# Five token blocks instead of six in a fused window-attention and two-FFN kernel, with the attention placed at quarters of a unit

## The chip, the cores and the metric

One core of a Trainium2 chip runs the whole program in one launch. The metric is the device time of that launch in microseconds (us); a time is the median of several runs. Engines are named as the profile names them: PE multiplies matrices (PEld loads its weights), DVE is the vector engine, ACT the scalar engine, POOL the third elementwise engine, SP issues most of the DMAs.

## The reference

4 sequences of 576 tokens, 8 heads of 64; a causal window of 64 keys; then two feed-forward nets over the 2304 tokens.

```python
scores = (q @ k.T) / sqrt(64)                  # per batch and head
scores = where(0 <= row - col < 64, scores, -1e9)
attn = softmax(scores)                         # max subtracted first
x = (attn @ v), heads side by side             # 2304 x 512
x = ((x @ w1) * (x @ w2) @ w3) @ w_out         # 512 -> 1024 -> 1024 -> 512
h = x @ w_in                                   # 512 -> 2048
out = (h * sigmoid(h)) @ w_out2                # 2304 x 512
```

## The kernel before

**Precision.** Most products are taken in three passes (`PASSES`): each operand is held as a high part and a low part, and PE adds high x high, high x low and low x high. So everything that feeds PE is copied (high part, on ACT) and subtracted (low part, on POOL or DVE). The weights come as float64 words and are turned into such pairs on the chip ("chunks", `steps_to`).

**Stages.** `phase_w` multiplies w3 and w_out into one 1024 x 512 matrix `wp`, so the first net is (a * b) @ wp. `phase_a(blk, hooks)` runs the first net for one block of tokens, `NB = 384` at a time, six blocks. It has 24 units of 12 matmuls. Units 0 to 15 make a = x@w1 and b = x@w2 in turn (line 520, tile `ab`): after an even unit ACT copies the accumulator into `a` (L526), after an odd one DVE multiplies (L528), ACT casts the product to its high part and POOL takes the low part (L79, L82, tiles `p` and `q`). Units 16 to 23 multiply by `wp` (line 540, tile `x`); ACT copies the result out and issues its DMA to the buffer `x2d`. The last block carries the conversion of the second net's weights. After it the second net runs over blocks of 512 tokens (L640, L659).

**Attention.** It is cut into 72 groups g, each 128 queries of two heads (18 token tiles of 128, 4 head pairs). A group is spread over six "halves" (`half(h)`); half 2g is its even one, 2g+1 its odd one. Even half 2g: PE takes the scores of g (L268 or L272, L276, tile `s`), multiplies the probabilities of group g-2 with the values (L349, L350, tile `o`) and transposes those of g-1 (L315, tile `t`). DVE adds the mask and takes the row minimum (L282, `sm`, `nm`), ACT copies the transposed probabilities of g-1 (L325, L327, `pt`), DVE takes their low parts (L328, L330), and ACT takes the exponentials of g (L293). Odd half 2g+1: DVE normalises g (L301, L303, L305), ACT and DVE add up group g-2's output (L357 to L360, `ot`) and POOL stores it (L361, `xr`), then q, k and v of later groups are split (L247, L251, L254, `qkhi`, `klo`, `vhl`). The first 17 groups (`plain`) take the scores in plain float32 with fewer of these steps.

**Order.** Nothing is scheduled automatically: each engine runs its instructions in the order in which the program emits them, and waits only for what an instruction needs. In `phase_w` 28 halves are emitted. In blocks 0 to 4 each of the 24 units emits one half ahead of its 12 matmuls (`halves_to(W_HALVES + 24 * blk + n + 1)`); in block 5 nothing is left. The tile `t` has one buffer, `sm` and `pt` have two. The next block's input is split out of `xr` during units 17 to 22 (`split_x`).

## Time and profile before

| | before |
|---|---|
| median of 3 runs | 861.66 us (861.57 to 862.0) |
| the profiled execution's own time | 861.8 us |
| its span in the trace | 860.0 us |
| PE busy | 842.0 us, 98% of the span |
| ACT, DVE, POOL busy | 497.7, 435.8, 445.0 us |
| `phase_w` (0 to 95.9 us) | PE busy 82.27 us of 96 |
| blocks 0 to 4 with attention (95.9 to 412.2) | a group every 5.25 us |
| block 5 (412.2 to 464.9), weights converted beside it | PE busy all of it |
| second net (464.9 to 860) | PE busy 391 us of 395 |

A row of the timeline gives start and length in us, engine, line, operation, what is written and read, and in brackets the idle time ahead of it with what ended it. The chain of waits is followed back from the last instruction: each piece is what the end of the program waited for at that time.

### The profile page before, as it was taken

What the parts mean: (1) busy time and instruction counts of PE and PEld (TensorE: products, weight loads), DVE (VectorE), ACT (ScalarE), POOL (GpSimd) and SP (SyncE); (2) the same over time, 40 slices, a digit from 0 to 9 for tenths busy, and PEclk for the clock granted to TensorE, in tenths of its full rate; (3) what the DMA queues carried; (4) which work ended last, traced back from release to release, by engine and by line L of the source; (5) the groups of instructions that cost most, each with busy time, mean ns of one, the idle gap of its engine ahead of it and who ended that gap; (6) DMA issues with size and microseconds to landing.
All of it is one profiled execution on the core that took longest, in us unless ns stands there. A gap on an engine that the chain in (4) does not pass through costs nothing.

```text
span 860.0 us, 13396 instructions
## 1 busy us (share of the span) xinstructions
PE 842.0 (98%) x4362; PEld 736.7 (86%) x4362; DVE 435.8 (51%) x1160; ACT 497.7 (58%) x1243; POOL 445.0 (52%) x494
## 2 busy tenths in 40 slices
PE   5899999999999999999999999999999999999998
PEld 2455799999999999999999888888888888888896
DVE  5979877677777777676465985111111111111111
ACT  5889778788788788787666874222222222222222
POOL 4668666566666666665595886223322232223222
PEclk9999999999999999999999999999999999999999
DMA  8988333333333334330687200200020002000100
GB/s 289 349 272 276 104 105 102 121 93 108 114 93 111 111 94 125 111 94 30 233 326 263 116 1 0 98 1 1 0 98 1 1 0 74 1 1 0 50 1 26
DMA packets 43205, 85.84 MB, mean 100 GB/s; under 512 B 4864, under 2 KB 22528, under 8 KB 43136
## 3 DMA queue, kind: packets, MB, share of 16 engines
q1 hardware_dynamic: 37088, 75.55, 26.7%
q10 hardware_dynamic: 6048, 9.44, 3.0%
q8 instruction: 35, 0.57, 0.3%
q14 instruction: 34, 0.28, 0.1%
HBM read 75.53 MB, written 9.44 MB: 99 GB/s over the span
## 4 chain that ended last, share of the span: by engine, by line
PE 86%; DVE 1%; ACT 1%; issue 1%; POOLq 0%; POOL 0%; ACTq 0%; DVEq 0%
PE h L640 23%; PE o L659 23%; PE ab L520 22%; PE x L540 12%; PE t L315 2%; PE o L349 1%; PE s L272 1%; PE s L276 1%; PE o L350 1%; ACT sm L293 0%; DVE a L528 0%; DVE sm L305 0%; DVE cv_b L128 0%; POOLq L765 0%; DVE hl L144 0%
## 5 line engine op out<-in xcount | busy, mean ns | idle before, releaser
L82 POOL TENSOR_TENSOR g<-sg,g 128x512 fp32r<-128x512 f32 (+1 forms) x80 | 94.7, 1184 | 244.8 <-ACT g L79 217.7
L640 PE MATMUL h<-x2t,hl 128*128 128x512 f32 (+1 forms) x960 | 210.1, 368 | 0.0
L659 PE MATMUL o<-hl,g 128*128 128x512 f32 x864 | 209.7, 390 | 0.1
L640 PEld LDWEIGHTS h<-x2t,hl 128*128 128x128 f32 x960 | 169.3, 188 | 31.2
L646 DVE TENSOR_TENSOR sg<-h,sg 128x512 f32<-128x512 f32 (+1 forms) x80 | 51.1, 638 | 283.7 <-ACT sg L645 283.6
L659 PEld LDWEIGHTS o<-hl,g 128*128 128x128 f32 x864 | 161.1, 188 | 33.5 <-POOL g L82 0.5
L645 ACT ACTIVATE sg<-h 128x512 f32<-128x512 f32 (+1 forms) x80 | 44.4, 555 | 190.0 <-PE h L640 189.7
L520 PE MATMUL ab<-xa,hl 128*128 128x384 f32 x576 | 119.0, 341 | 0.0
L520 PE MATMUL ab<-xb,hl 128*128 128x384 f32 x576 | 115.3, 334 | 0.0
L520 PEld LDWEIGHTS ab<-xb,hl 128*128 128x128 f32 x576 | 101.2, 188 | 0.0
L520 PEld LDWEIGHTS ab<-xa,hl 128*128 128x128 f32 x576 | 99.2, 188 | 0.0
L132 POOL TENSOR_TENSOR cv_b<-cv_b,cv_r 128x512 int32<-128x512 int32 x48 | 73.5, 1531 | 19.1 <-DVE cv_b L128 8.1
L79 ACT CAST g<-sg 128x512 fp32r<-128x512 f32 (+1 forms) x80 | 46.3, 579 | 63.5 <-DVE sg L646 63.5
L361 POOL TENSOR_TENSOR xr<-ot 128x128 f32<-128x128 f32 x55 | 31.6, 575 | 98.3 <-DVE ot L360 67.2
L251 POOL TENSOR_TENSOR klo<-qk,qkhi 64x192 fp32r<-64x192 f32 x110 | 67.4, 613 | 7.6 <-ACT qkhi L247 2.7
L540 PE MATMUL x<-p,wp 128*128 128x384 f32 x360 | 68.0, 339 | 0.0
L293 ACT ACTIVATE sm<-sm,nm 128x192 f32<-128x192 f32 x144 | 64.5, 450 | 3.9 <-DVE nm L282 2.5
L540 PEld LDWEIGHTS x<-p,wp 128*128 128x128 f32 x360 | 61.7, 188 | 0.1
L125 DVE TENSOR_SCALAR cv_z<-cv_b 128x512 int32<-128x512 int32 x72 | 49.4, 686 | 15.7 <-ACT cv_b L114 14.7
L114 ACT ACTIVATE cv_b<-words 128x512 f32<-128x512 f32 x72 | 48.3, 671 | 12.2 <-DMA words<-in_w_out 4.6
L128 DVE SCALAR_TENSOR_TENSOR cv_b<-words,cv_z 128x512 int32<-128x512 int32 x72 | 49.5, 687 | 3.3
L115 ACT ACTIVATE cv_r<-words 128x512 int32<-128x512 uint32 x72 | 47.8, 664 | 0.0
(81 smaller groups left out, 1236.5 us busy)
## 6 DMA issues: line engine op xcount, KB each, us to landing
qk<-in_qkv SPq DMA_DIRECT2D x55, 384.0 KB, 3.1
words<-in_w_out SPq DMA_DIRECT2D x24, 512.0 KB, 8.0
words<-in_w3t SPq DMA_DIRECT2D x16, 512.0 KB, 6.4
words<-in_w SPq DMA_DIRECT2D x16, 512.0 KB, 6.4
words<-in_w_in SPq DMA_DIRECT2D x16, 512.0 KB, 6.7
v<-in_qkv SPq DMA_DIRECT2D x55, 96.0 KB, 2.7
x2d<-x2s ACTq DMA_DIRECT2D x24, 192.0 KB, 1.9
out_x<-osb ACTq DMA_DIRECT2D x18, 256.0 KB, 2.1
```

Source lines behind the costliest of these rows:

```text
L82: (nc.vector if eng_lo == "dve" else nc.gpsimd).tensor_tensor(out=lo, in0=src, in1=f32(hi), op=ALU.subtract)
L114: nc.scalar.activation(out=f32(self.b), in_=f32(self.high), func=AF.Copy, scale=2.0**-112)
L125: nc.vector.tensor_scalar(out=self.z, in0=b, scalar1=3, scalar2=None, op0=ALU.logical_shift_left)
L128: nc.vector.scalar_tensor_tensor(out=b, in0=self.high, scalar=-0x80000000, in1=self.z, op0=ALU.bitwise_and, op1=ALU.bitwise_or)
L132: nc.gpsimd.tensor_tensor(out=x, in0=b, in1=self.r, op=ALU.add)
L251: nc.gpsimd.tensor_tensor(out=k_lo[g % 2][hs, h * 192 : h * 192 + 192], in0=t[hs, n], in1=f32(hi[hs, n]), op=ALU.subtract)
L293: nc.scalar.activation(out=x, in_=x, func=AF.Exp, scale=-1.0, bias=nm[:, h : h + 1], accum_out=sums_of[g % 2][:, h, 0:1])
L520: nc.tensor.matmul(acc, lhsT=w[:, l, fs], rhs=x[k // 2][:, k % 2, r, :], start=(k == 0 and n == 0), stop=(k == 3 and n == 2),)
L540: nc.tensor.matmul(acc, lhsT=wp[f][:, l, o * 128 : (o + 1) * 128], rhs=p[f][:, r, :], start=(f == 0 and n == 0), stop=(f == 7 and n == 2),)
L640: nc.tensor.matmul(acc, lhsT=weights["in", f // 4, k][:, l, fs], rhs=x[:, k, r, :], start=(k == 0 and i == 0), stop=(k == 3 and i == 2),)
L646: nc.vector.tensor_tensor(out=sg, in0=acc, in1=sg, op=ALU.mult)
L659: nc.tensor.matmul(oacc[t], lhsT=g[:, l, t * 128 : (t + 1) * 128], rhs=weights["out", f][:, r, :], start=(f == 0 and i == 0), stop=(f == 1 ...
```

## The change

**Blocks.** `UNITS = (3, 3, 4, 4, 4)` gives five blocks of 384, 384, 512, 512 and 512 tokens instead of six of 384. Every matmul of `phase_a` in the last three is 512 columns wide, and the slots `p`, `q`, `xa`, `xb` and `xr` grow to 512 columns. To make room, `klo` and `kp` share one slot each (`klo` is allocated and zeroed on POOL when the first split group needs it, in block 0), and plain and split values share one.

**Halves.** The 120 halves that were 24 in each of five blocks are now 28, 28, 32 and 32 in four (`HALVES_AT`), and none in the last. They are placed at quarters of a unit, that is ahead of every 3 matmuls, by `attend(n, k)`.

**Order inside the halves.** In the even half the exponentials of g are emitted ahead of the copies of g-1's probabilities. The low parts of g-1 move to the odd half, behind the normalising of g.

```diff
-        def unit(n):
-            halves_to(W_HALVES + 24 * blk + n + 1)
+        def attend(n, k):
+            halves_to(begun + min(ahead, -(-ahead * (4 * n + k + 1) // (96 if blk == 0 else 92))))
+
+        def unit(n):
+            attend(n, 0)
             hooks(n)
...
             for k in range(4):
                 w = weights["12", (2 * m + f // 4) * 4 + k]
+                if k:
+                    attend(s, k)
...
-            if 1 <= g <= NG:
-                split_t(g - 1, transposes(g - 1))
+            t_ps = transposes(g - 1) if 1 <= g <= NG else None
             if g < NG:
                 exps(g)
+            if t_ps is not None:
+                lows.append(split_t(g - 1, t_ps))
...
             if g < NG:
                 normalise(g)
+            if lows:
+                lows.pop()()
             if sums:
                 sums.pop()()
```

The blocks are counted from 0. PE in block 1, units 2 and 3, before. The names: `s`, `o` and `t` are scores, values and transposes, `ab` the products with w1 or w2.

```order
L315 MATMUL t_1972<-id_sb,sm_72 128x128 x3
L520 MATMUL ab_2_1984<-xa_1638,hl 128x384 x6
L520 MATMUL ab_2_1984<-xb_1639,hl 128x384 x6
L520 MATMUL ab_3_2020<-xa_1638,hl 128x384 x6
L520 MATMUL ab_3_2020<-xb_1639,hl 128x384 x6
L272 MATMUL s_2036<-qkhi_1932 128x192 x2
L276 MATMUL s_2036<-klo_74,qkhi_1932 128x384
L349 MATMUL o_2044<-pt_975,vhl_1937 128x256 x2
L350 MATMUL o_2044<-pt_973,vhl_1937 128x4x64
L315 MATMUL t_2048<-id_sb,sm_73 128x128 x3
L520 MATMUL ab_4_2060<-xa_1638,hl 128x384 x6
```

The rows of one group stand behind unit 3 there. PE in block 1 after, units 3 and 4:

```order
L329 MATMUL t_2140<-id_sb,sm_73 128x128 x3
L548 MATMUL ab_3_2124<-xa_1718,hl 128x384 x3
L548 MATMUL ab_3_2124<-xb_1719,hl 128x384 x6
L548 MATMUL ab_4_2185<-xa_1718,hl 128x384 x6
L548 MATMUL ab_4_2185<-xb_1719,hl 128x384 x3
L286 MATMUL s_2195<-qkhi_2101 128x192 x2
L290 MATMUL s_2195<-klo_1111,qkhi_2101 128x384
L367 MATMUL o_2203<-pt_982,vhl_2106 128x256 x2
L368 MATMUL o_2203<-pt_980,vhl_2106 128x4x64
L329 MATMUL t_2207<-id_sb,sm_72 128x128 x3
L548 MATMUL ab_4_2185<-xb_1719,hl 128x384 x3
```

The attention's five rows stood between whole units, 24 matmuls from one group to the next; now they stand inside unit 4, 18 matmuls after the last ones.

DVE in block 1 before, from the second row minimum of a group (`nm`) to the multiply of unit 7 (`a_3`); `rs` and `sm` are the normalising, `pt` the low parts, `ot` the output sums.

```order
L282 ISA sm_73,nm_2116<-s_2112,mask_sb 128x192
L282 ISA nm_2116 128x1
L328 TENSOR_TENSOR pt_975<-t_2124,pt_975 128x2x128
L330 TENSOR_TENSOR pt_973<-t_2124,pt_973 64x64 x2
L301 TENSOR_REDUCE rs_2117<-es_82 128x2
L303 RECIPROCAL rs_2117<-rs_2117 128x2
L305 TENSOR_TENSOR sm_73<-sm_73,rs_2117 128x384
L359 TENSOR_TENSOR ot_2154<-o_2120,ot_2154 64x256
L360 TENSOR_TENSOR ot_2154<-o_2120,ot_2154 64x256
L254 TENSOR_TENSOR qkhi_2160<-qk_2016,qkhi_2160 64x256
L528 TENSOR_TENSOR a_3_2149<-ab_7_2172,a_3_2149 128x384
```

The low parts stand ahead of the normalising there. DVE in block 1 after, from the second row minimum to the multiply of unit 5 (`a_2`):

```order
L296 ISA sm_73,nm_2199<-s_2195,mask_sb 128x192
L296 ISA nm_2199 128x1
L315 TENSOR_REDUCE rs_2200<-es_77 128x2
L317 RECIPROCAL rs_2200<-rs_2200 128x2
L319 TENSOR_TENSOR sm_73<-sm_73,rs_2200 128x384
L344 TENSOR_TENSOR pt_981<-t_2207,pt_981 128x2x128
L346 TENSOR_TENSOR pt_979<-t_2207,pt_979 64x64 x2
L377 TENSOR_TENSOR ot_2237<-o_2203,ot_2237 64x256
L378 TENSOR_TENSOR ot_2237<-o_2203,ot_2237 64x256
L267 TENSOR_TENSOR qkhi_2243<-qk_2109,qkhi_2243 64x256
L556 TENSOR_TENSOR a_2_2219<-ab_5_2221,a_2_2219 128x384
```

The two rows of low parts have moved from ahead of the three of normalising to behind them; the multiply still stands at the end of this group's rows here.

ACT in block 1 before, from one cast of a product (`p`) to the next; `pt` are the copies, `sm` the exponentials.

```order
L79 CAST p_1882<-a_2_2073 128x384
L325 CAST pt_975<-t_2124 128x2x128
L327 CAST pt_973<-t_2124 64x64 x2
L293 ACTIVATE sm_73,es_82<-sm_73,nm_2116 128x192 x2
L526 COPY a_3_2149<-ab_6_2136 128x384
L357 COPY ot_2154<-o_2120 64x256
L358 COPY ot_2154<-o_2120 64x256
L247 CAST qkhi_2160<-qk_2016 128x768
L79 CAST vhl_2165<-v_1942 128x3x64
L79 CAST p_1882<-a_3_2149 128x384
```

The exponentials stand behind the copies there. ACT in block 1 after, from the exponentials of one group to those of the next:

```order
L307 ACTIVATE sm_73,es_77<-sm_73,nm_2199 128x192 x2
L339 CAST pt_981<-t_2207 128x2x128
L341 CAST pt_979<-t_2207 64x64 x2
L554 COPY a_2_2219<-ab_4_2185 128x384
L375 COPY ot_2237<-o_2203 64x256
L376 COPY ot_2237<-o_2203 64x256
L260 CAST qkhi_2243<-qk_2109 128x768
L90 CAST vhl_2248<-v_2041 128x3x64
L90 CAST p_1986<-a_2_2219 128x384
L307 ACTIVATE sm_72,es_76<-sm_72,nm_2272 128x192 x2
```

The exponentials stood behind the three copies into `pt`; now they stand ahead of them.

## Rows read from the trace of the kernel before

**Rows 1.** The page, parts 1 and 6: busy us; loads with KB and us to landing.

```profile
PE 842.0 (98%) x4362; PEld 736.7 (86%) x4362; DVE 435.8 (51%) x1160; ACT 497.7 (58%) x1243; POOL 445.0 (52%) x494
...
qk<-in_qkv SPq DMA_DIRECT2D x55, 384.0 KB, 3.1
```

**Rows 2.** The chain in order of time: start us, length us, what.

```profile
235.06 4.17 PE ab L520 x24
...
412.21 33.28 PE ab L520 x192
...
475.83 2.72 PE h L640 x12
...
814.67 1.43 PE h L640 x12
```

**Rows 3.** Line 82, who waited for it: us, times. (POOL's low parts.)

```profile
PEld x L540: 1.2, 4
```

**Rows 4.** Timeline of DVE, block 2: one round of a group.

```profile
235.15 0.56 DVE L528 TENSOR_TENSOR a<-ab,a 128x384 f32<-128x384 f32 x1
235.63 0.35 DVE L282 CUSTOM_DVE_ANT_0 sm<-s,mask_sb 128x192 f32<-128x192 f32 x1
...
236.90 0.42 DVE L328 TENSOR_TENSOR pt<-t,pt 128x256 fp32r<-128x256 f32 x1 [0.64 <-ACT pt L327]
237.24 0.45 DVE L330 TENSOR_TENSOR pt<-t,pt 64x64 fp32r<-64x64 f32 x2
237.91 0.16 DVE L301 TENSOR_REDUCE rs<-es 128x2 f32<-128x4 f32 x1 [0.22 <-ACT sm L293]
...
238.31 0.56 DVE L305 TENSOR_TENSOR sm<-sm,rs 128x384 f32<-128x384 f32 x1
239.24 0.42 DVE L359 TENSOR_TENSOR ot<-o,ot 64x256 f32<-64x256 f32 x1 [0.38 <-ACT ot L358]
...
240.03 0.42 DVE L254 TENSOR_TENSOR qkhi<-qk,qkhi 64x256 fp32r<-64x256 f32 x1
240.48 0.56 DVE L528 TENSOR_TENSOR a<-ab,a 128x384 f32<-128x384 f32 x1
```

**Rows 5.** The same stretch on ACT.

```profile
235.75 0.52 ACT L79 CAST p<-a 128x384 fp32r<-128x384 f32 x1 [0.83 <-DVE a L528]
236.17 0.36 ACT L325 CAST pt<-t 128x256 fp32r<-128x256 f32 x1
...
236.89 0.46 ACT L293 ACTIVATE sm<-sm,nm 128x192 f32<-128x192 f32 x1
...
237.90 0.48 ACT L526 COPY a<-ab 128x384 f32<-128x384 f32 x1
...
238.40 0.37 ACT L357 COPY ot<-o 64x256 f32<-64x256 f32 x1
...
239.16 0.83 ACT L247 CAST qkhi<-qk 128x768 fp32r<-128x768 f32 x1
```

**Rows 6.** The same stretch on PE: scores and values.

```profile
239.06 0.37 PE L272 MATMUL s<-qkhi 128*128 128x192 f32 x2
239.27 0.36 PE L276 MATMUL s<-klo,qkhi 128*128 128x384 f32 x1
239.46 0.39 PE L349 MATMUL o<-pt,vhl 128*128 128x256 f32 x2
```

**Rows 7.** Timeline of block 2, units 18 and 19: POOL and DVE at once.

```profile
274.28 1.02 POOL L82 TENSOR_TENSOR xa<-xr,xa 128x384 fp32r<-128x384 f32 x1
...
274.95 0.77 DVE L305 TENSOR_TENSOR sm<-sm,rs 128x384 f32<-128x384 f32 x1
```

**Rows 8.** Timeline of the start of block 0, conversions beside it: POOL, DVE, PE.

```profile
95.03 0.20 POOL L556 MEMSET pt<- 64x128 f32 x1
...
112.04 0.98 DVE L305 TENSOR_TENSOR sm<-sm,rs 128x384 f32<-128x384 f32 x1
...
113.17 0.52 PE L315 MATMUL t<-id_sb,sm 128*128 128x128 f32 x3 [0.30 <-DVE sm L305]
```

More of the change, by code (lines that the diff above doesn't have):

```diff
@@ L22 @@
 DM, FF, FF2 = 512, 1024, 2048
-NB = 384
-NBLK = T // NB
 NU = T // 128
+UNITS = (3, 3, 4, 4, 4)
+NBLK = len(UNITS)
+FIRST = [sum(UNITS[:b]) for b in range(NBLK + 1)]
+NBM = max(UNITS) * 128
 NPAIR = H // 2
@@ L32, with place @@
 W12_BY = [n * W12_A // 8 for n in range(8)] + [W12_A + n * (W12_B - W12_A) // 8 for n in range(8)]
+def place(g):
+    b = max(n for n in range(NBLK) if FIRST[n] * NPAIR <= g)
+    c, r = divmod(g - FIRST[b] * NPAIR, UNITS[b])
+    return b, FIRST[b] + r, c
 def mask_kind(u):
@@ L193, in tile_window_attention_ffn @@
     sm = [att.tile([128, 2, 192], F32, name=f"sm{i}", tag=f"sm{i}", bufs=1) for i in range(2)]
-    k_lo = [att.tile([128, 384], F32R, name=f"klo{i}", tag=f"klo{i}", bufs=1) for i in range(2)]
-    k_p = [att.tile([128, 384], F32, name=f"kp{i}", tag=f"kp{i}", bufs=1) for i in range(2)]
-    v_p = [att.tile([128, 320], F32, name=f"vp{i}", tag=f"vp{i}", bufs=1) for i in range(3)]
+    k_p = [att.tile([128, 384], F32, name=f"kp{i}", tag=f"k{i}", bufs=1) for i in range(2)]
+    k_lo = {}
     sums_of = [
@@ L219, in load_qk @@
             loaded.add(g)
-            u, c = place(g)
+            _, u, c = place(g)
             if not plain(g):
@@ L234, in load_v, with zero_beside @@
             loaded.add(("v", g))
+            v_raw[g] = att.tile([128, 320], F32, name=f"v{g}", tag="v", bufs=3)
             if plain(g):
-                nc.sync.dma_start(out=v_p[g % 3], in_=vp[g])
+                nc.sync.dma_start(out=v_raw[g], in_=vp[g])
                 return
-            v_raw[g] = att.tile([128, 3, 64], F32, name=f"v{g}", tag="v", bufs=3)
-            u, c = place(g)
-            nc.sync.dma_start(out=v_raw[g].rearrange("p t d -> p (t d)"), in_=qkv[u, c, :, 768:960])
+            _, u, c = place(g)
+            nc.sync.dma_start(out=v_raw[g][:, 0:192], in_=qkv[u, c, :, 768:960])
+    def zero_beside(t):
+        for h, hs in HEADS:
+            nc.gpsimd.memset(t[hs, 192 - h * 192 : 384 - h * 192], 0.0)
     def prep_qk(g):
@@ L245, in prep_qk @@
         t = qk_raw.pop(g)
+        if g % 2 not in k_lo:
+            k_lo[g % 2] = att.tile([128, 384], F32R, name=f"klo{g % 2}", tag=f"k{g % 2}", bufs=1)
+            zero_beside(f32(k_lo[g % 2]))
         hi = att.tile([128, 768], F32R, name=f"qkhi{g}", tag="qkhi", bufs=2)
@@ L327, in split_t, with low @@
             nc.scalar.copy(out=a[hs, h, 0], in_=before[hs])
-        nc.vector.tensor_tensor(out=b[:, :, 1, :], in0=own, in1=f32(b[:, :, 0, :]), op=ALU.subtract)
-        for h, hs in HEADS:
-            nc.vector.tensor_tensor(out=a[hs, h, 1], in0=before[hs], in1=f32(a[hs, h, 0]), op=ALU.subtract)
+        def low():
+            nc.vector.tensor_tensor(out=b[:, :, 1, :], in0=own, in1=f32(b[:, :, 0, :]), op=ALU.subtract)
+            for h, hs in HEADS:
+                nc.vector.tensor_tensor(out=a[hs, h, 1], in0=before[hs], in1=f32(a[hs, h, 0]), op=ALU.subtract)
+        return low
     def values(g):
-        u, c = place(g)
-        r = u % 3 * 128
+        b, u, c = place(g)
+        r = (u - FIRST[b]) * 128
         tag = "z" if done["step"] == len(line) and g % 2 else "o"
@@ L399, in half @@
                 load_v(x)
-    halves, sums = [0], []
+    halves, sums, lows = [0], [], []
     def halves_to(n):
```

57 lines of the change are left out of this document (31 added, 26 removed).

## The prediction

> **What bounds the kernel now.** I read the page's busy times first, then the chain of waits in order of time, then the timeline of one round of attention on DVE, ACT and PE. PE is busy 842.0 of 860.0 us [rows 1], and from block 0 to the end the chain is PE's own queue with hardly a gap, so the time is a sum of matmuls, and a change pays only in what PE executes or waits for. The reader should see in [rows 2] that a matmul's price is nearly linear in its columns with a fixed part: 2.72/12 = 0.2267 us at 512, 33.28/192 = 0.1733 at 384, 1.43/12 = 0.119 at 256. Each step of 128 columns is 0.053 to 0.054, so some 0.013 us are paid for each matmul however wide it is.
>
> The second thing to see is a loop that PE does not show. PE passes a group of attention every 5.25 us (24 matmuls, 4.17 us [rows 2], and 1.08 of attention). DVE's multiply of the products starts at 235.15 and next at 240.48 [rows 4]: the round of ACT and DVE takes 5.33. Its links are the cast of the product at 235.75, the copies of the probabilities from 236.17, the exponentials from 236.89, the accumulator's copy from 237.90, the output copies from 238.40, the cast of q and k from 239.16 [rows 5], and DVE's q low part from 240.03 to the next multiply at 240.48 [rows 4]. In the units with products the loop is already slower than PE by 0.08 us a group, and PE does not feel it because there is slack and because the eight other units have no multiply. Whatever makes attention denser must shorten this loop.
>
> **Part 1, wider blocks.** Six blocks of 288 matmuls at 0.1733 are 1728 x 0.1733 = 299.5 us. After: 576 x 0.1733 + 864 x 0.2267 = 99.8 + 195.9 = 295.7. All of it lies on PE's path: **-3.8 us**, with bounds -3.5 and -4.0 from the roundings. The second net is untouched. The Trainium skill (TensorE: Matmul & The Clock Gate, Back-to-back issue gap) gives an isolated matmul N/2.4 ns plus 2.5. By that the 288 matmuls saved would be worth only 0.7 us; the trace disagrees, with a fixed part of some 13 ns at three widths, and the rows decide.
>
> **Part 2, the wait ahead of `x`.** POOL's low part of the last products makes PE's weight load wait 1.2 us in 4 waits [rows 3], one in each of four blocks. After the change a group of attention (1.08 us) stands between the last product and the matmul that needs its low part, which covers a wait of 0.3; but where DVE lags, the product comes late and the wait stays. From -1.2 to 0: **-0.6**.
>
> **Part 3, denser attention.** The budget of a group: in block 1, 92 quarters for 14 groups are 19.7 matmuls, 3.42 + 1.08 = 4.50 us. In block 0, 96 quarters: 4.65. In blocks 2 and 3, 92 for 16 at 512 columns: 17.25 x 0.2267 + 1.08 = 4.99. Against that the new loop, put together by hand from starts of [rows 4, 5], from one group's last exponential to the next one's:
> - through DVE: normalising 0.96 (237.91 to the end at 238.87), low parts 0.79 (236.90 to 237.69), output sums 0.79, q's low part 0.45, row minimum 0.35, exponentials 1.01: 4.35; with a product's multiply in between 0.48 more (235.15 to 235.63), 4.83;
> - through ACT: copies 0.72, a cast or accumulator copy 0.42 to 0.50, output copies 0.76, cast of q and k 0.87, then DVE's 0.45 and 0.35, exponentials 1.01: 4.6; with the multiply, and the cast that waits for it ahead of the exponentials, 5.1 to 5.3.
>
> So the new order does shorten the loop, from 5.33 to some 4.5 without and 5.15 with a multiply. In the order of block 1 ten groups pass beside the sixteen product units. Four of them have the multiply behind the q low part, inside the loop (`a_2`, `a_3`, `a_6`, `a_7`); the others have it in the gap in which DVE waits for the exponentials. Mean: (6 x 4.5 + 4 x 5.15)/10 = 4.76, 0.26 over the budget, 2.6 us for ten groups.
>
> Against it stands the slack. Scores are ready 0.57 after their start (239.06 to 239.63 [rows 6]); row minimum, exponentials, normalising and low parts follow: 0.57 + 0.35 + 1.01 + 0.96 + 0.79 and some 0.1 of handing over make 3.8. The next group's values need the low parts at 4.50 + 0.40 = 4.90 (values start 0.40 behind scores [rows 6]). The slack is 1.1, and PE waits some 1.5 us in block 1. What is queued behind that wait on PE is everything: transposes, then the products.
>
> Block 0: 4.76 against 4.65 is inside the slack, but the early units also carry conversions. There PE waits 0.30 for the normalising already, at the old cadence, and the normalising multiply takes 0.98 in place of 0.56 [rows 8]. With the first three groups some 0.5 to 1.0 us closer, less the copy that the exponentials no longer wait for, I take 1.0 for the wait and nothing for the rest (from 0 to 2.5). `klo`'s zeroing adds four operations of about 0.20 [rows 8] on POOL ahead of its low parts of k; they are due more than a group later, so nothing, at most 0.8. Blocks 2 and 3: casts and multiply grow by at most a third, which gives a mean of some 4.9 against 4.99: 0.2 for each. Eight lighter units a block and collisions between POOL and DVE add perhaps 0.8 (second rival). Sum of PE's new waits: 1.5 + 1.0 + 0.4 + 0.8 = 3.7, less the old 0.3: **+3.4**, from 0 to +9.
>
> **At nothing.** In `phase_w` the exponentials come one copy earlier; that shifts DVE and ACT by less than the 0.72 of three copies [rows 5] either way, and I take 0. The loads per group keep their order on SP and are issued two groups ahead; they land in 3.1 us [rows 1], inside one group even at 4.50. The last block has the same conversions and more PE time to hide them. The stores of `x2` on ACT become 20 instead of 24.
>
> **Sum.** -3.8 - 0.6 + 3.4 = -1.0 on the profiled execution's 861.8 (span 860.0 and 1.8 around it), which stands 0.1 over the median: **860.7 us**.
>
> **The rivals.**
> 1. *The loop stays hidden* (faster). For it: eight units of each block have no multiply, block 1's last quarter-unit steps are free of halves, and the slack may be taken up only late. Then PE waits only in block 0: -3.8 - 1.2 + 0.7 = -4.3, that is 857.4; with half of the expected waits 858 to 859.9. Chance 0.36.
> 2. *POOL and DVE collide* (slower). In [rows 7] POOL's low part runs from 274.28 to 275.30 and the normalising multiply, started at 274.95, ends 0.42 behind it: 0.77 in place of 0.56. In the product units of before POOL happens to be free at that point; with rounds of 6 or 7 quarters against units of 4 the two drift across each other. The multiply stands in the loop, so 0.3 a group over the 24 groups of blocks 0 and 1 passing at 4.50 to 4.65 is up to 7 more, some 5 with what the lighter units absorb: about 865. It decides from 0.12 a group (24 x 0.12 = 2.9): above that the change is slower than before by over 0.2%. Against it: POOL is busy only 445.0 of 860 us [rows 1], and it is DVE's output sum that lets it start on the next group. Chance 0.22. The Trainium skill (SBUF — State Buffer, SBUF: two separate sides) calls the read and write port pair that DVE shares with GpSimd an exclusive lock, held for a whole instruction by whoever starts first; [rows 7] agree, since DVE's operation ends a fixed part after POOL's.
> 3. *Fewer matmuls save nothing.* If the 0.013 belonged to the columns and not to the matmul, 288 x 0.013 = 3.7 of part 1 would be gone: 864.4. Three widths in [rows 2] speak against it: 0.02. The rule of the Trainium skill named in part 1 would come out near this.
>
> **How the numbers follow.** About 0.2%, 1.7 us, is what a measurement of this kernel tells from no change. Within it (859.9 to 863.4): my forecast, PE's new waits eating most of the gain, 0.40. Faster: 0.36. Slower: 0.22 + 0.02 = 0.24. The range reaches to the first rival's 857.4 and to nearly all of the second: 857.4 to 864.8. The forecast's own range is 859.9 to 863.4.
>
> **What would show it.** `ab` and `x` matmuls of 0.227 us apart in blocks 2 to 4: part 1. Waits of PE at values or transposes (`o`, `t`) for DVE's `pt` or `sm`, near `a_2`, `a_3`, `a_6`, `a_7` of block 1: part 3; none there, and groups 4.50 apart: the first rival. Normalising multiplies well over the 0.56 us of [rows 4] in the mean: the second. I would be wrong altogether if PE waits in the last block or in the second net, or if `phase_w` ends more than a microsecond off 95.9.

## The result, and the profile after

The changed kernel takes **873.66 us** in the median (871.75 to 874.78), the kernel before 861.64 on the same chip: 1.0138 times as long, with an interval from 1.0125 to 1.015. I had forecast 860.7 and a range from 857.4 to 864.8. The change is slower by 1.4%, outside the range. The trace is that of the shortest of the four executions, 871.75 us, so it shows 10 of the 12 us; where the other 2 go was not traced.

The page of the changed kernel, part 1, answers to [rows 1]:

```profile
span 870.0 us, 12725 instructions
...
PE 844.9 (97%) x4074; PEld 700.7 (81%) x4074; DVE 443.1 (51%) x1152; ACT 489.9 (56%) x1219; POOL 444.5 (51%) x482
```

PE executes 288 matmuls less. The span is 10.0 us longer; PE stands still for 25.1 us in place of 18.0, and the rest of the loss hides in its busy time (behind a wait its next matmuls take longer, the values below 0.47 in place of 0.39). DVE is busy 7 us longer with fewer operations, and its 72 normalising multiplies alone take 57.1 us in place of 45.1 (lines below). That is the first trace of the cause.

The windows from a block's first `ab` matmul to the next one's, changed kernel (columns: length, then busy us and instructions of PE, PEld, DVE, ACT and POOL, granted clock, DMA):

```profile
95.07:168.82 73.75, 68.81 (x428) 66.70 (x426) 57.05 (x178) 58.22 (x173) 48.87 (x65) 1.00 0.36 108
168.82:239.57 70.75, 68.11 (x417) 65.80 (x416) 56.12 (x191) 57.82 (x178) 46.66 (x71) 1.00 0.36 110
239.57:324.20 84.63, 84.35 (x436) 71.93 (x434) 64.21 (x220) 66.83 (x200) 54.79 (x78) 1.00 0.35 106
324.20:406.66 82.46, 82.22 (x418) 69.79 (x416) 57.33 (x193) 60.45 (x182) 46.65 (x66) 1.00 0.30 93
406.66:474.82 68.16, 68.16 (x302) 56.47 (x301) 28.93 (x41) 36.55 (x64) 40.54 (x31) 1.00 0.57 210
```

By the prices of the prediction, a block of 384 tokens with 14 groups is 49.9 + 14 x 1.08 = 65.0 us of matmuls (block 0 some 1.6 more, since its first groups are plain ones), one of 512 with 16 groups is 65.3 + 17.3 = 82.6. Blocks 0, 1 and 2 are 8.7 (7.1 without those 1.6), 5.7 and 2.0 us longer than that; block 0 of before was 2.2 us longer than its 62.9 and block 1 only 0.4. PE's waits in the whole of the changed kernel, for values (`o`), transposes (`t`) and `x` (us in total, times, longest):

```profile
PE o L367 <- DVE pt L344: 7.2, 10, 2.4
PE t L329 <- DVE sm L319: 1.9, 4, 0.6
...
PE x L570 <- POOL q L93: 0.3, 1, 0.3
```

In the same list of before there is not one wait of PE for `pt`. The last block has no attention, and there the width paid. Its chain (start, length, what):

```profile
406.82 43.52 PE ab L548 x192
450.34 16.32 PE x L570 x72
...
469.38 5.44 PE x L570 x24
```

That is 0.2267 us a matmul, to the fourth digit what [rows 2] gave at 512 columns.

Now the round that sets the time. DVE in block 1, one group in a unit with a product (line 556 the product's multiply, 296 the row minimum, 315 to 319 normalising, 344 and 346 the probabilities' low parts, 377 and 378 the output sums):

```profile
212.90 0.56 DVE L556 TENSOR_TENSOR a<-ab,a 128x384 f32<-128x384 f32 x1
213.38 0.35 DVE L296 CUSTOM_DVE_ANT_0 sm<-s,mask_sb 128x192 f32<-128x192 f32 x1
...
214.93 0.16 DVE L315 TENSOR_REDUCE rs<-es 128x2 f32<-128x4 f32 x1 [0.92 <-ACT sm L307]
...
215.32 1.16 DVE L319 TENSOR_TENSOR sm<-sm,rs 128x384 f32<-128x384 f32 x1
216.41 0.41 DVE L344 TENSOR_TENSOR pt<-t,pt 128x256 fp32r<-128x256 f32 x1
216.74 0.44 DVE L346 TENSOR_TENSOR pt<-t,pt 64x64 fp32r<-64x64 f32 x2
217.21 0.42 DVE L377 TENSOR_TENSOR ot<-o,ot 64x256 f32<-64x256 f32 x1
...
218.44 0.56 DVE L556 TENSOR_TENSOR a<-ab,a 128x384 f32<-128x384 f32 x1
```

The same stretch on POOL, and PE's rows for the scores and the values that wait:

```profile
212.61 0.57 POOL L379 TENSOR_TENSOR xr<-ot 128x128 f32<-128x128 f32 x1 [2.09 <-DVE ot L378]
213.16 1.26 POOL L264 TENSOR_TENSOR klo<-qk,qkhi 64x192 fp32r<-64x192 f32 x2
214.50 0.60 POOL L93 TENSOR_TENSOR vhl<-v,vhl 128x192 fp32r<-128x192 f32 x1
215.05 1.01 POOL L93 TENSOR_TENSOR q<-a,q 128x384 fp32r<-128x384 f32 x1
```

```profile
215.60 0.37 PE L286 MATMUL s<-qkhi 128*128 128x192 f32 x2
...
216.96 0.47 PE L367 MATMUL o<-pt,vhl 128*128 128x256 f32 x2 [0.80 <-DVE pt L344]
```

Three things are to be seen. From multiply to multiply the round is 218.44 - 212.90 = **5.54** us, longer than the 5.33 of [rows 4], in a block that gives it 4.50. Not every round is so long: over the ten groups beside the product units of block 1 the mean is 5.02 (row minima from 173.74 to 223.96), in the old order 4.81 (`a_old_order` below, 170.64 to 218.76). The normalising multiply takes 1.16 us in place of 0.56: it starts 0.27 behind POOL's low part of the product and ends 0.42 after that one's end (216.06). And PE's values wait for the low parts of line 344, which now come last.

### The profile page after: what moved, and what is told of

The parts are those of the page before. It is cut to its first block, busy times and chain, and to the rows that moved or that the text cites. A ratio compares the mean times of both kernels' runs of the same rounds, so it can differ in the third digit from the quotient of the medians.

```text
span 870.0 us, 12725 instructions
## 1 busy us (share of the span) xinstructions
PE 844.9 (97%) x4074; PEld 700.7 (81%) x4074; DVE 443.1 (51%) x1152; ACT 489.9 (56%) x1219; POOL 444.5 (51%) x482
## 4 chain that ended last, share of the span: by engine, by line
PE 70%; DVE 7%; issue 5%; ACT 4%; POOL 2%; DMA 0%; POOLq 0%; ACTq 0%; DVEq 0%
PE h L670 22%; PE o L689 22%; PE ab L548 11%; PE x L570 10%; ACT sm L307 2%; PE t L329 1%; PE o L367 1%; DVE a L556 1%; DVE sm L296 1%; DVE ot L378 1%; DVE pt L344 1%; DVE qkhi L267 1%; DVE ot L377 1%; PE o L368 1%; PE s L286 1%
## 5 line engine op out<-in xcount | busy, mean ns | idle before, releaser
L548 PE MATMUL ab<-xb,hl 128*128 128x512 f32 (+1 forms) x480 | 115.8, 372 | 0.0
L548 PE MATMUL ab<-xa,hl 128*128 128x512 f32 (+1 forms) x480 | 115.6, 372 | 0.0
L548 PEld LDWEIGHTS ab<-xa,hl 128*128 128x128 f32 x480 | 86.5, 188 | 10.7
L548 PEld LDWEIGHTS ab<-xb,hl 128*128 128x128 f32 x480 | 86.4, 188 | 10.7
L379 POOL TENSOR_TENSOR xr<-ot 128x128 f32<-128x128 f32 x55 | 31.3, 570 | 80.9 <-DVE ot L378 70.3
L570 PE MATMUL x<-p,wp 128*128 128x512 f32 (+1 forms) x300 | 67.1, 371 | 0.0
L570 PEld LDWEIGHTS x<-p,wp 128*128 128x128 f32 x300 | 54.1, 188 | 6.9
L319 DVE TENSOR_TENSOR sm<-sm,rs 128x384 f32<-128x384 f32 x72 | 57.1, 793 | 2.5
```

Of the source, the lines that this page charges most:

```text
L319: nc.vector.tensor_tensor(out=x, in0=x, in1=rs.unsqueeze(2).to_broadcast([128, 2, 192]), op=ALU.mult)
L548: nc.tensor.matmul(acc, lhsT=w[:, l, fs], rhs=x[k // 2][:, k % 2, r, :], start=(k == 0 and n == 0), stop=(k == 3 and n == 2),)
L570: nc.tensor.matmul(acc, lhsT=wp[f][:, l, o * 128 : (o + 1) * 128], rhs=p[f][:, r, :], start=(f == 0 and n == 0), stop=(f == 7 and n == 2),)
```

## The experiments

The lengths that I read from each kernel's timeline of PE stand in one table, from a block's first `ab` matmul to the next block's. "Multiply" is the mean of the 72 normalising multiplies (before: 45.1 us in all, 0.627), "1st phase" the end of `phase_w`. All but the median is read from one execution of each kernel.

```
                         median  1st phase  block 0  block 1  block 2  block 3  multiply
changed kernel           873.66    95.07     73.75    70.75    84.63    82.46    0.793
a_old_order              863.12    96.07     70.34    67.54    83.43    81.24    0.633
a_no_low                 867.35    94.28     73.10    69.35    83.46    81.30    0.666
a_v_later                878.22    97.00     75.87    72.06    85.85    83.94    0.655
a_lows_only              873.78    96.08     73.68    71.13    85.05    82.95    0.679
a_exps_only              899.17    95.72     77.40    79.34    91.56    89.81    0.634
a_no_special             872.71    98.14     72.17    70.58    84.89    82.47    0.816
c_old_32                 864.03    99.06     68.22    65.37    83.42    81.25    0.660
d_old_defer              862.29    95.42     69.92    67.26    83.44    81.24    0.638
d_new_defer              870.01    97.34     73.77    69.28    83.48    81.28    0.692
e_low_dve                869.38    95.72     74.21    69.30    83.47    81.31    0.660
f_best                   862.10    94.76     68.91    67.58    83.43    81.24    0.655
six blocks: before       861.64    95.89     65.10    63.32    63.30    63.28    0.627
            b_new_order  868.77    96.62     65.62    64.87    64.85    64.84    0.927
            b_dense      891.29    95.16     73.71    72.82    71.78    74.92    0.771
            e_six_defer  862.88    98.41     65.28    63.52    63.52    63.55    0.765
```

The end of the first phase scatters from 94.3 to 98.4 us among kernels with the same first phase, so differences are read from the blocks.

My theory after the result: the new order of the operations inside a group, not the denser attention by itself, is the cause, since it puts the normalising under POOL's low part and makes the round longer. The rival: attention is too dense at 4.5 us, in any order.

### The order undone, and the order alone

`a_old_order`, the changed kernel with the old order:

```diff
-            t_ps = transposes(g - 1) if 1 <= g <= NG else None
+            if 1 <= g <= NG:
+                split_t(g - 1, transposes(g - 1))()
             if g < NG:
                 exps(g)
-            if t_ps is not None:
-                lows.append(split_t(g - 1, t_ps))
```

> The changed kernel with the order inside a group as it was before the change (probability copies and low parts ahead of the exponentials); widths and quarters stay. Theory A (the attention of ACT and DVE takes longer than the time between two groups, and the new order shortens it): PE's waits at values grow from the 7 to 8 us of the changed kernel, blocks 0 and 1 become longer than 74.0 and 70.8 us, the time is 878 to 890. Theory B (it is the new order that puts the normalising multiply under POOL's low part): the multiply falls from 0.79 us in the mean to about 0.6, blocks 0 and 1 return to 67 to 69 us, the time is 860 to 867.

863.12 us, 1.0019 times before (1.0009 to 1.0028). Blocks 0 and 1 return to 70.3 and 67.5, part of the way, and blocks 2 and 3 nearly wholly. Over blocks 0 to 3 the new order costs 311.59 - 302.55 = 9.04 us. That is theory B, with block 0 above what it expected.

`b_new_order`, the other way round: six blocks, the old cadence, the new order (and the shared buffers of the change).

```diff
-UNITS = (3, 3, 4, 4, 4)
+UNITS = (3,) * 6
...
-    HALVES_AT = (W_HALVES, 56, 84, 116, 148, 148)
+    HALVES_AT = (W_HALVES, 52, 76, 100, 124, 148, 148)
...
-            halves_to(begun + min(ahead, -(-ahead * (4 * n + k + 1) // (96 if blk == 0 else 92))))
+            halves_to(begun + min(ahead, -(-ahead * (4 * n + k + 1) // 96)))
```

> Six blocks of 384 tokens and halves at the units as before the change; the new order inside a group, and the shared buffers for v and k, are the only differences. Theory A (cadence): with 5.25 us from group to group there is slack, so within 0.2% of the kernel before, 860 to 863, blocks 63.3 apart. Theory B (order): the normalising multiply rises from 0.61 to 0.7 us or more, PE waits at values or transposes, 864 or more.

868.77 us, 1.0083 (1.0068 to 1.0099): theory B. At a cadence of 5.25 us, where the old order loses 0.4 a block, the new one loses 1.55 us more in each of blocks 1 to 3 (0.5 in block 0). PE's list of waits holds only 0.5 us of that in all; the rest is spread over spacings too small for the list, so the block lengths are the measure. The multiply over the whole kernel, out of the groups by line (busy us, mean ns), of before, of the changed kernel, of `a_old_order` and of `b_new_order`:

```profile
L305 DVE TENSOR_TENSOR sm<-sm,rs 128x384 f32<-128x384 f32 x72 | 45.1, 627 | 2.5
```

```profile
L319 DVE TENSOR_TENSOR sm<-sm,rs 128x384 f32<-128x384 f32 x72 | 57.1, 793 | 2.5
```

```profile
L319 DVE TENSOR_TENSOR sm<-sm,rs 128x384 f32<-128x384 f32 x72 | 45.6, 633 | 2.5
```

```profile
L319 DVE TENSOR_TENSOR sm<-sm,rs 128x384 f32<-128x384 f32 x72 | 66.7, 927 | 2.5
```

Why the order decides it is seen from a chain that starts on DVE. The output sums release POOL, which then takes its four operations in a row: sum 0.58, k's low parts 1.27, v's 0.60, the product's 1.01, together 3.45 us of work, which ends 3.52 to 3.54 us after the sums. In the old order the normalising multiply starts 3.53 us after them; `a_old_order`, DVE and then POOL:

```profile
213.54 0.56 DVE L555 TENSOR_TENSOR a<-ab,a 128x384 f32<-128x384 f32 x1
...
215.28 0.42 DVE L344 TENSOR_TENSOR pt<-t,pt 128x256 fp32r<-128x256 f32 x1 [0.63 <-ACT pt L341]
...
216.69 0.56 DVE L319 TENSOR_TENSOR sm<-sm,rs 128x384 f32<-128x384 f32 x1
```

```profile
215.15 0.60 POOL L93 TENSOR_TENSOR vhl<-v,vhl 128x192 fp32r<-128x192 f32 x1
215.70 1.00 POOL L93 TENSOR_TENSOR q<-a,q 128x384 fp32r<-128x384 f32 x1
```

POOL ends at 216.70 as the multiply starts at 216.69. Before the change it is the same: in the round of [rows 4] the sums end at 234.77, the multiply starts at 238.31, and POOL ends at 238.33:

```profile
237.31 1.02 POOL L82 TENSOR_TENSOR p<-a,p 128x384 fp32r<-128x384 f32 x1
```

Of the 72 multiplies of before, 37 start in the last 0.04 us of an operation of POOL, and all 37 take 0.56. In the new order copies and low parts no longer stand ahead of the normalising, it starts 2.78 us after the sums, and POOL is 0.27 us into the product's low part. `b_new_order`, DVE and then POOL, a round that repeats 5.52 to 5.55 us apart through the product units:

```profile
245.16 0.16 DVE L315 TENSOR_REDUCE rs<-es 128x2 f32<-128x4 f32 x1 [0.92 <-ACT sm L307]
...
245.55 1.15 DVE L319 TENSOR_TENSOR sm<-sm,rs 128x384 f32<-128x384 f32 x1
```

```profile
245.28 1.01 POOL L93 TENSOR_TENSOR p<-a,p 128x384 fp32r<-128x384 f32 x1
```

So the two do not drift across each other: the distance is fixed by the order, and the collision comes in every round that follows a product's multiply.

### Cadence alone

`b_dense`: six blocks, new order, and 28 halves in each of blocks 0 to 3 at quarters (`HALVES_AT = (W_HALVES, 56, 84, 112, 140, 148, 148)`). Its attention runs more than one block ahead of the buffer `xr`, so that the later blocks read another block's values; all the operations are there.

> Six blocks of 384 tokens, new order, but 28 halves in each of blocks 0 to 3 at quarters of a unit and 8 in block 4: the cadence of the changed kernel's blocks 0 and 1 without any width of 512. Theory A (cadence): block 0 as in the changed kernel, 74, blocks 1 to 3 some 5.6 us of waits each, 70 to 71, block 4 shorter than 61: 861.6 + 7.4 + 3 x 5.6 = about 885 (880 to 889). Rival (the loss comes from the widths, from casts and multiplies a third longer, or from the first two blocks alone): blocks 1 to 3 at most 67, 868 to 873.

891.29 us, blocks 1 to 3 of 71.8 to 74.9: as theory A said, and more. The width of 512 is not needed for the loss. What stood unsaid in the expectation is that this kernel has the new order too, so it shows dense attention in the new order, no more.

### The colliding operation

`a_no_low` leaves POOL's low part of the product out:

```diff
-                split(p[f][:, 0], p[f][:, 1], a_sb[:, 1], "act", "pool")
+                nc.scalar.copy(out=p[f][:, 0], in_=a_sb[:, 1])
...
-                        acc, lhsT=wp[f][:, l, o * 128 : (o + 1) * 128], rhs=p[f][:, r, :],
+                        acc, lhsT=wp[f][:, l, o * 128 : (o + 1) * 128], rhs=p[f][:, 0, :],
```

> The changed kernel without POOL's low part of the products (16 operations of about 0.8 to 1 us a block); PE reads the high part in its place, so that its matmuls are as many and as wide. Collision theory (POOL's low part holds up the normalising multiply of DVE, which stands in the loop): the multiply falls from 0.79 to about 0.6 in the mean, PE's waits at values in blocks 0 and 1 fall to under half, blocks 0 and 1 take 69 to 70 and 66 to 67.5, the time is 862 to 867. Cadence alone (the loop is too long with or without collisions): 870 to 873, blocks 0 and 1 over 72 and 69.5.

867.35 us, the multiply 0.666 (over 0.6, so some of the collisions remain, with other operations of POOL): the collision is real, and over blocks 0 to 3 it is worth 311.59 - 307.21 = 4.4 us. But block 0 stays at 73.1, where the other case had it (over 72), and block 1 at 69.35, longer than with the old order. So there is a second price. In block 0 a part of it is one wait of 2.40 us at the block's end, of which more below.

`e_low_dve` keeps the work and puts the operation on DVE, behind the next row minimum, where DVE waits for the exponentials anyway:

```diff
+            if late and halves[0] % 2:
+                late.pop()()
...
-                split(p[f][:, 0], p[f][:, 1], a_sb[:, 1], "act", "pool")
+                nc.scalar.copy(out=p[f][:, 0], in_=a_sb[:, 1])
+                beside = s < 15 and halves[0] % 2 == 0
+                low = partial(
+                    (nc.vector if beside else nc.gpsimd).tensor_tensor,
+                    out=p[f][:, 1], in0=a_sb[:, 1], in1=f32(p[f][:, 0]), op=ALU.subtract,
+                )
+                if beside:
+                    late.append(low)
+                else:
+                    low()
```

> The changed kernel with all its work, but a product's low part on DVE, behind the next row minimum (in the time in which DVE waits for the exponentials), when the half before was an odd one; otherwise and for a block's last product on POOL as before. If POOL's low part of the product is a real part of the price: the normalising multiply under 0.68 us in the mean, 866 to 869, about as without that operation (867.4). If taking it away only paid because work was left out: the multiply falls and the time stays, 871 to 875, since DVE has 0.45 us more to do in a round.

869.38 us (1.0088, from 1.0064 to 1.0111), the multiply 0.660, and blocks 1 to 3 equal to those of `a_no_low` within 0.05. So the gain does not come from work left out. The median is 0.4 above the expected range, and block 0 is no shorter than in the changed kernel.

`a_v_later` tried to clear POOL by issuing v's cast and low part half a group later:

```diff
                 lows.append(split_t(g - 1, t_ps))
+                prep_v(g - 1)
...
-            if g < NG:
-                prep_v(g)
```

> The changed kernel, all its work kept; only v's cast and low part are issued half a group later (behind the probability copies), and v's load one group later, so that POOL comes to the product's low part 0.6 us earlier and is through with its chain (output sum 0.58, k low parts 1.27, product low part 1.01: 2.9 us behind DVE's output sums) when the normalising multiply starts, 2.8 us behind them. Collision by order (POOL's fixed chain lies under the multiply since the low parts stand behind it): the multiply falls from 0.79 to about 0.62 us, the time to 865 to 869, as without the product's low part (867.4). If the collision is a drift of phases that no order changes: the multiply stays at 0.75 or more and the time within 872 to 875.

A miss. The multiply fell to 0.655 as the order said it would, and the time rose to 878.22. PE's waits for values from the first block on show the price:

```profile
PE o L367 <- POOL vhl L93: 6.1, 10, 1.1
PE o L367 <- DVE pt L344: 3.5, 2, 3.2
```

v's low part now came just when PE needs it, and v's cast on ACT stood ahead of the output copies; the longest rounds of block 1 stayed at 5.5 to 5.6 nearly without a collision (multiplies of 0.56 to 0.61 in them, one of 0.83). Moving one operation out of the way put another into the loop.

### The two halves of the reordering

`a_lows_only` has the copies ahead of the exponentials as before, the low parts behind the normalising as after:

```diff
-            t_ps = transposes(g - 1) if 1 <= g <= NG else None
+            if 1 <= g <= NG:
+                lows.append(split_t(g - 1, transposes(g - 1)))
             if g < NG:
                 exps(g)
-            if t_ps is not None:
-                lows.append(split_t(g - 1, t_ps))
```

> The changed kernel with one half of its reordering: probability copies ahead of the exponentials as before the change, the probabilities' low parts behind the normalising multiply as after it. The multiply starts 0.72 us later behind the output sums than in the changed kernel (about 3.5 us), when POOL's chain of 3.45 us has just ended. Theory 1 (the collision is the whole price of the new order): multiply about 0.6 us, 863 to 867. Theory 2 (the low parts, 0.85 us, no longer lie in the shadow of the exponentials, and a group's values come later by them): multiply about 0.6 to 0.65 us, and yet 873 or more, since the loop is 5.33 + 0.6, with PE's waits at values for the low parts over 8 us in all.

873.78 us, the time of the changed kernel, with a multiply of 0.679 in place of 0.793: theory 2, though the multiply is above and the waits for the low parts (7.6) are below what it said. Its longest rounds of block 1 measure 5.66 us with a multiply of 0.56 in them, 0.33 more than in the old order, where theory 2 had 0.6. PE's waits from the end of the first phase on:

```profile
PE o L367 <- DVE pt L344: 7.6, 11, 1.4
```

`a_exps_only` has the exponentials ahead of the copies, and the low parts right behind the copies, ahead of the normalising (`split_t(g - 1, t_ps)()` in place of `lows.append(...)`).

> The changed kernel with the other half of its reordering: the exponentials ahead of the probability copies as after the change, the probabilities' low parts right behind their copies and ahead of the normalising multiply as before it. Theory 1 (the loop of ACT and DVE decides; in the old order it measures 5.33 us from row minimum to row minimum with a product's multiply in it, in the new one 5.54 with the collision): here the copies (0.72) and low parts (0.85) stand one behind the other between exponentials and normalising, the loop is 5.7 to 5.9, PE waits at transposes for the normalising, not at values, 872 to 882. Theory 2 (only the low parts' late place is bad, since PE needs them 1.3 us earlier within a group than the normalised matrix): at most 866, like the old order.

899.17 us: theory 1 in kind, the size far beyond it. Exponentials, copies, low parts and normalising now stand one behind the other, rounds take 5.0 to 6.2 us in blocks 1 and 2, in all kinds of units, and from 85 to 420 us PE waits 44 times, now for the normalising:

```profile
PE t L329 <- DVE sm L319: 26.5, 44, 1.3
```

So neither half of the reordering pays by itself; together they cost what the first costs, and far less than the second. In the old order the low parts lie beside the exponentials, which ACT is busy with anyway; both halves give that up.

### The multiply in the round

From row minimum to row minimum, one kernel's DVE timeline shows three kinds of rounds: a product's multiply stands right ahead of both row minima, of one of them, or of neither (it may then lie beside the exponentials). The first and the last column are from blocks 0 and 1, the first also from the product units of before and `b_new_order`; the last has the shortest rounds, and the middle one is block 1:

```
                              at both ends   at one end     at neither
old order                         5.33       4.47 to 4.85      4.47
new order                         5.54       5.05 to 5.13      4.57
new order, a_no_low               5.19       4.72 to 5.13      4.57
```

At six blocks nearly all rounds of the product units are of the first kind. At the changed kernel's cadence block 1 has two of them, and four at one end.

`d_old_defer` and `d_new_defer` issue a product's multiply, cast and low part behind the next even half when the half before was an odd one (`product` appends the three operations to `late` as one step):

```diff
+            if late and halves[0] % 2:
+                late.pop()()
...
-                nc.vector.tensor_tensor(out=a_sb[:, 1], in0=acc, in1=a_sb[:, 0], op=ALU.mult)
-                split(p[f][:, 0], p[f][:, 1], a_sb[:, 1], "act", "pool")
+                product(p[f], a_sb, acc)
+                if s == 15 or halves[0] % 2:
+                    late.pop()()
```

> Five blocks at quarters with the old order inside a group, and one edit against the multiply in the loop: a product's multiply, cast and low part are issued behind the next even half (behind row minimum, low parts and exponentials) when the half before it was an odd one; the last product of a block stays at its place. In the run with the old order rounds took 5.33 us from row minimum to row minimum with the multiply ahead of it and 4.47 without or with the multiply beside the exponentials. If these 0.86 us are what blocks 0 and 1 (70.3 and 67.5 us, against 66.6 and 65.1 without waits) lose: rounds of 4.5 to 4.6, block 1 at 65.1 to 66, block 0 at 67 to 69, the time 858.5 to 861.5. If the loss comes from elsewhere: 862.5 to 865.

862.29 us, 1.0008 (0.9996 to 1.0019), no difference from before. The time lies between the two cases; the blocks speak for the second, for blocks 0 and 1 gain only 0.3 to 0.4 over `a_old_order`. The rounds did not become 4.5 to 4.6: over the ten groups beside the product units of block 1 the mean is 4.78 (169.58 to 217.42), against 4.81. The deferred cast now stands ahead of ACT's output copies, and DVE waits 1.06 us for them at 187.60. So deferring moved the multiply's cost in the old order; what that cost is, the run does not show.

> The changed kernel with the same edit (multiply, cast and low part of a product behind the next even half). If the multiply in the loop, together with the collision that its low part on POOL brings, is what makes the new order lose: rounds of 4.6 instead of 5.54, collisions on the normalising few (mean under 0.65), block 1 at 66 to 67.5, the time 863 to 867. If the late low parts of the probabilities are enough to lose (less slack, whatever the round): over 869, blocks 0 and 1 over 72 and 69.

870.01 us, the second case, with a multiply of 0.692, more than the first expected. Blocks 0 to 3 gain 3.8 us over the changed kernel, but against `d_old_defer`, which differs in the order alone, they are still 307.81 - 301.86 = 6.0 us longer: 3.85 in block 0, 2.0 in block 1, next to nothing in blocks 2 and 3. Block 0 still has the changed kernel's longest wait, at its end:

```profile
159.40 0.77 PE L367 MATMUL o<-pt,vhl 128*128 128x256 f32 x2 [2.40 <-DVE pt L344]
```

The same wait of 2.40 stands in `a_no_low` and, with 2.41, in `e_low_dve`, and not in `a_old_order` or `d_old_defer`. So what looks like the price of the late low parts is in part this one place, the subject of `a_no_special` below.

`e_six_defer` puts the same edit into `b_new_order`, six blocks at the old cadence.

> Six blocks of 384, the new order, the old cadence of 5.25 us, and a product's multiply, cast and low part issued behind the next even half. If the 7 us that the new order costs at the old cadence come from its round of 5.54 us, longer than 5.25: rounds of 4.6 to 5.0, blocks 63.3 apart again, 861 to 863. If they come from the late place of the low parts alone: blocks stay at 64.5 or more, over 866.

862.88 us, 1.0013 (1.0001 to 1.0026), and the blocks are back, here block 1:

```profile
163.69:227.21 63.52, 63.38 (x400) 63.09 (x398) 47.92 (x165) 51.80 (x157) 40.46 (x61) 1.00 0.34 107
```

Its rounds in the product units are 5.24 to 5.26 us apart but for the last, at PE's pace, with multiplies of 0.73 to 0.80 in place of 1.16, and the late low parts cost next to nothing. It has the shared buffers too, so they are not what `b_new_order` lost by. What the new order loses at the old cadence it loses through the length of its round; the late low parts are a price only where attention is dense.

### Places at the blocks' ends, and more attention in the first phase

The longest wait of the changed kernel, 2.40 us at values near 158.6, is at the end of block 0, where the output sum of the block's last group is taken half a group early and DVE waits behind it for ACT's output copies. `a_no_special` drops this in blocks 0 to 2 (in block 2 the sum then comes behind its use, and that unit reads old values).

> The changed kernel without the early output sum at a block's last group in blocks 0 to 2 (it is done half a group later, as in any other group, and still ahead of its use). If that early sum makes the 2.40 us wait of PE at values near 158.6, which it does by putting DVE behind ACT's output copies: that wait goes, block 0 is 71.1 to 71.5 in place of 73.8, the time 870.5 to 871.5. If the low parts are late there anyway: under 1 us less, 872.7 to 874.

872.71 us. Block 0 gains 1.6, where 2.3 to 2.7 were expected, block 2 gives 0.3 back, and the time is 1 us shorter: by the time the second case, by block 0 between the two. The early sum is a part of what made that wait; PE's longest wait for `pt` is now 1.0.

`c_old_32`: the old order, and 32 halves beside the first phase (`HALVES_AT = (W_HALVES, 58, 84, 116, 148, 148)`).

> Five blocks with the old order inside a group, and 32 halves (two groups of attention more, in their plain form) beside the first phase, so that blocks 0 and 1 have 26 halves each (5.0 and 4.8 us from group to group in place of 4.65 and 4.50). If the remaining 4.7 and 3.0 us that blocks 0 and 1 lose with the old order come from the cadence: both lose under 1.5, which is worth 5 to 6, against 2 to 4 for the plain groups in the first phase: 859 to 862. If they come from the start of the split groups and the block's end instead: 864 to 867.

864.03 us. Blocks 0 and 1 become 2.1 and 2.2 us shorter, of which 1.08 each is a group less, so the waits gave about 1.1 each; and the first phase is 3.0 longer in the traced execution. By the prices above `a_old_order` is 3.7 and 2.5 over its matmuls in blocks 0 and 1 (the 4.7 and 3.0 of the expectation are too high), and this kernel 2.7 and 1.4. The time is at the lower edge of the second case.

`f_best`: `d_old_defer` without the early sum in block 0, and with the matmul that needs the last product's low part moved behind two products of the next chain.

```diff
+                    if (o, f, n) == (0, 7, 1):
+                        continue
...
+                if (o, f) == (1, 1):
+                    nc.tensor.matmul(first, lhsT=wp[7][:, 0, 0:128], rhs=p[7][:, 1, :], start=False, stop=True)
+                    store(0, first)
```

> Five blocks at quarters, the old order, multiply, cast and low part of a product behind the next even half (862.3 so far), and two edits: in the first chain of x the matmul that needs the last product's low part comes behind the next chain's second product, and the early output sum at the end of the next block's groups is dropped in block 0. If the waits of 1.05 us (x for POOL's low part, 1.3 with its refill, in block 1 and in part in others) and 0.8 (transposes at the end of block 0) are what is left: both gone, 859.5 to 861. If the same lag turns up at the next group instead: 861.5 to 863.

862.10 us, 1.0013 (0.9997 to 1.0029): the second case. In `a_old_order` and `d_old_defer` PE waited there for POOL (0.86 and 1.05); in `f_best` that row is gone and the next group waits instead. `a_old_order`, then `f_best`:

```profile
216.75 0.44 PE L569 MATMUL x<-q,wp 128*128 128x384 f32 x1 [0.86 <-POOL q L93]
```

```profile
214.36 0.52 PE L329 MATMUL t<-id_sb,sm 128*128 128x128 f32 x3 [0.80 <-DVE sm L319]
```

No version beat the kernel before.

## Why the prediction was wrong, point by point

**What bounds the kernel** held: PE's queue is the chain, and a change pays in what PE executes or waits for. The last block's 0.2267 us apart show it.

**Part 1, -3.8: right.** 0.2267 at 512 and 0.1733 at 384 stood, and with them the third rival fell. The saving itself is worked out from these spacings; no run has the width alone.

**Part 2, -0.6: right.** By the row of [rows 3] PE's weight load now waits 0.6 us once, in place of 1.2 in four; in PE's own list above the same wait is 0.3.

**Part 3, +3.4: this is the step that failed.** From the first `ab` to the first `h` behind the last `x` the kernel before takes 368.9 us, `a_old_order` 370.5, the changed kernel 379.6. With the 3.8 of part 1 put back, the dense attention costs 1.7 + 3.8 = 5.5 in the old order, and the new order 9.0 on top. So parts 2 and 3 together measured 14.5, where I had 2.8 and, for part 3, an upper bound of 9. Block 0 lost 7.1 where I had 1.0, block 1 5.7 against 1.5, block 2 2.0 against 0.2. Which four multiplies stand in the loop of block 1 was right (the four that start ahead of a row minimum there, at 187.75, 193.30, 212.90 and 218.44, are `a_2`, `a_3`, `a_6` and `a_7`), and PE's longer waits of that block, 0.87, 0.43 and 0.80, stand behind `a_2`, `a_3` and `a_6`. What failed is the length of the round: the mean of 4.76, 0.26 over the budget, measured 5.02, 0.52 over it. Three errors made it so.
- *The round does not get shorter.* I had it shrink from 5.33 to 5.15 with a multiply, and set 4.5 without one against the same 5.33. The right pairs are 5.33 against 5.54 and 4.47 against 4.57, and the mean of the ten groups of block 1 grew from 4.81 to 5.02. A round of the old order without the multiply was in the trace of before, the first behind each block's last product, 4.49 to 4.51 from row minimum to row minimum, and I did not look. The hand-made 5.1 to 5.3 for the new round with a multiply was right without a collision (5.19 in `a_no_low`).
- *The collision is not a drift.* I took 0.3 a group where POOL and DVE happen to meet, and wrote that in the product units POOL "happens to be free". It is free by next to nothing, and by construction: its chain ends 3.52 to 3.54 us after the output sums, and the normalising starts 3.53 after them. The reorder takes 0.75 out of the second. The multiply then takes 0.6 more (1.16 against 0.56) in every round that follows a product's multiply and runs by its own pace, and the round at both ends 0.35 more (5.54 against 5.19).
- *The slack is smaller.* I worked out 1.1 us and let the lag eat it. With 0.6 of collision in the 3.8 us it is 0.5 (an estimate), and in block 1 two rounds lag 1.04 (5.54 - 4.50) and four about 0.55.

**At nothing.** The first phase ended 0.8 us earlier, within its scatter. One zero was wrong: at a block's end the early output sum stands ahead of the normalising on DVE; together with the new order it made the single longest wait, 2.40. In before the same sum is there, and PE has no wait for `pt` behind it.

**The rivals.** The first (hidden loop) is refuted by the waits. The second named the mechanism, and its sign (normalising multiplies well over 0.56) came true with 0.793; its 865 was too low, as it took the collision for an addition of at most 0.3 to a round that was otherwise short enough. Its 0.22 was too little for a mechanism whose row stood in the trace.

**What stays open.** How the 6.0 us between `d_new_defer` and `d_old_defer` divide into the wait at the end of block 0, the slack that the late low parts take elsewhere, the collisions that are left (0.692 against 0.638) and the 0.1 of a longer round was not taken apart; no run has the deferred multiply in the new order without the early sum. That the cost of 5.5 of the dense attention in the old order lies in the start of the split groups in block 0 and in the last product of block 1 is read from rows; removing two of its waits moved the lag and did not end it.

## What to carry to other kernels

When a reorder brings an operation forward, measure its distance from the event that also starts its neighbours' chain, here 3.53 us against POOL's 3.54; two engines released by the same operation keep their phase, and a near miss in the old order is a hit in the new one. Compare rounds of the same kind, with and without the extra operation, and look for each in the trace of before. Work that lies beside another engine's wait is free only as long as it stays there: moved to the round's end it costs its length and the consumer's slack.

## What the runs showed of the hardware

A multiply on DVE with both inputs in SBUF that starts while POOL works on SBUF ends 0.41 to 0.45 us behind POOL's operation, wherever in it it began: 1.16 us when it started 0.27 behind the start of a 1.01 us one, 0.77 in [rows 7]; 49 of the 72 normalising multiplies of the changed kernel show it. One that starts in the last 0.1 us keeps its 0.56. DVE's operations that read one input from PSUM, the probabilities' low parts, keep their 0.42 us beside POOL's work (215.28 in `a_old_order`, with POOL busy from 215.15 to 215.75), and POOL's own 1.01 does not change where it started first. Where the multiply started first, POOL is the one that is longer: 1.38 us for 384 columns of `xb` that start 0.05 behind it (159.57 in `a_old_order`). The Trainium skill (SBUF — State Buffer, SBUF: two separate sides) names the same condition for its lock, two SBUF inputs on DVE against a POOL operation that reads SBUF, and the trace agrees on both sides. I had not expected that the first phase, the same instructions in the same order, ends anywhere from 95.07 (changed kernel) to 98.14 us (`a_no_special`).
